# Reordering the first 13 microseconds of a fused adaLN, attention and MLP kernel, and moving TensorE's branch behind its last matmul

## Chip, cores, metric

One core of one Trainium2 chip. The metric is device microseconds of the whole launch. Engines in profile lines: PE is TensorE (PEld its weight loads), DVE is VectorE, ACT is ScalarE, POOL is GpSimd, SP is SyncE; a "q" behind the name is the engine's sequencer. Tiles in them: st, mv and rstd are row statistics, tmp and sc_bf the steps of silu, xn normalized rows, modc scale and shift, hT the transposed input of q, PT the output rows, wmw weights (in the opening those of w_mod); psQ, psS, psO and psW are TensorE's output banks. Dummies are psW<-ones, and a psO ahead of q.

## The reference, cut to what matters

```python
mod = (silu(c) @ w_mod).reshape(1, 6, 1, 512)        # c: 512 values, w_mod: 512 x 3072
sa, ca, ga, sb, cb, gb = (mod[:, i] for i in range(6))
h = layernorm(x) * (1 + ca) + sa                     # x: 2048 x 512, bf16
x = x + ga * attention(h, k_cache, v_cache, wq, wo)  # 32 heads of 128, 8 kv heads, last 512 keys
h = layernorm(x) * (1 + cb) + sb
out = x + gb * (relu(h @ w1) @ w2)                   # 512 -> 1792 -> 512
```

Before the first attention score, four things must have happened for the first 512 rows of x: the row statistics, the normalization (tiles 0 to 3, 128 rows each), the products of w_mod with silu(c), and q = h @ wq. That is the **opening**. From then on TensorE streams matmuls to the end.

## The kernel before

Each engine has its own list of operations; a helper works out the semaphore waits between them. The dummy matmuls, `warm`, only keep TensorE busy so that its clock turns up. The opening, cut:

```python
    warm(7)                                   # 7 dummies of 512 columns
    silu_exp(5)                               # TensorE transposes c; ScalarE: exp(-c) and a copy
    warm(9)
    # ... ScalarE: mean and variance of tile 3
    silu_mul()                                # GpSimd: 1 + exp(-c), its power -1, the product with c
    ln_stat(0); ln_stat(1)                    # VectorE
    rstd_add(0, 2); rstd_pow(0, 2)            # VectorE, then GpSimd: (var + eps) ** -0.5
    ln_stat(2); rstd_add(2, 3); rstd_pow(2, 4)
    ln_norm(0); ln_norm(1)                    # VectorE; tile 3 is normalized by GpSimd
    ln_tposes(0, TB[0])                       # TensorE: four 128 x 128 transposes
    for f in mod_cols_mm(0, QBK): f()         # TensorE: 32 products of one column
    ln_norm(2)
    mod_cols_evac(0, QBK)                     # VectorE: scale and shift out of PSUM
    for tl in range(1, TPB): ln_tposes(tl, TB[tl // 2])
    mod_half(0, 0, DVE); mod_half(0, 2, ACT)  # a piece of hT: transposed tiles * scale + shift
    # ... the other pieces of hT, 16 q matmuls in halves, copies to SBUF
```

Once, late in the program, every engine reads a flag (was the softmax safe without its maximum?) and branches: either the rest of its fast list, or a general kernel of thousands of instructions that lies in between in the program:

```python
            def engine(name, e):
                stream, n_ops = fast[name], cut[name]
                kb.emit(stream, e, 0, n_ops)
                e.wait_ge(sems[flag_ev[0]], flag_ev[1])
                v = e.value_load(flag[0:1, 0:1])
                with e.If(v != 128):
                    # ... the rest, then the whole general kernel
                with e.Else():
                    kb.emit(stream, e, n_ops)
```

TensorE's `cut` stood two groups before the end of the third block of the MLP, at about 510 us.

## Time and profile before

| | before |
|---|---|
| time | 560.52 us median of 3 runs (560.2 to 560.57) |
| span of the profiled run | 559.4 us (this run timed at 561.1 us) |
| TensorE busy | 98% of the span |
| first q matmul | 10.86 us |
| copy of the first q ends | 12.98 us |
| last matmul starts | 556.47 us |
| issue of the last output to its landing | 1.49 us |

The opening and the tail are read in the chain and in the timeline; in between, TensorE's stream is one block.

### The profile page before, as it was taken

The numbers are of one execution on the slowest core, as the hardware profiler recorded it, in microseconds if no ns is written. First come the engines' busy times: TensorE is split into PE (matmuls) and PEld (weight loads), VectorE is DVE, ScalarE is ACT, GpSimd is POOL, SyncE is SP. The second block draws the span as 40 slices with busy tenths as digits, with TensorE's granted clock in tenths as the row PEclk, the third lists the DMA queues.
The fourth block names the chain that finished last, engine by engine and source line by source line (L and its number), as shares of the span: only waits on it lengthen the run. The fifth ranks groups of instructions, "written<-read, shape, count | busy, mean of one in ns | idle before, by whom it ended". The sixth has DMA issues, their size and how long they took to land.

```text
span 559.4 us, 9666 instructions
## 1 busy us (share of the span) xinstructions
PE 550.5 (98%) x4060; PEld 315.8 (56%) x4134; DVE 253.8 (45%) x551; ACT 348.9 (62%) x453; POOL 54.7 (10%) x53
## 2 busy tenths in 40 slices
PE   8999999999999999999999999999999999999998
PEld 4665555555555555555555555555555654444444
DVE  4455555553546544335445443333354448321134
ACT  4986666666666666666666666666666644432500
POOL 3000022004410000033000000332000000000000
DMA  9897763513114144352352412111215110210001
GB/s 268 248 207 174 143 169 46 114 39 76 40 38 76 39 73 117 58 133 57 94 95 57 76 40 39 39 39 38 39 39 76 39 30 0 44 34 23 22 29 47
DMA packets 113309, 42.67 MB, mean 76 GB/s; under 512 B 93928, under 2 KB 112104, under 8 KB 113256
## 3 DMA queue, kind: packets, MB, share of 16 engines
q1 hardware_dynamic: 112024, 40.82, 34.3%
q10 hardware_dynamic: 1232, 1.15, 0.6%
q8 instruction: 33, 0.54, 0.4%
q14 instruction: 20, 0.16, 0.1%
HBM read 18.35 MB, written 2.10 MB: 37 GB/s over the span
## 4 chain that ended last, share of the span: by engine, by line
PE 98%; issue 1%; DMA 1%; DVE 0%; SPq 0%; DVEq 0%
PE psS L1372 28%; PE psO L1372 27%; PE psQ L1372 23%; PE psW L1372 20%; DMA c_row<-in_c_dram 1%; DVE qT L1611 0%; DVE hT L1630 0%; SPq L1303 0%; DVE PT L1723 0%; DVE PT L1725 0%; PE psS L1375 0%; PE psO L1416 0%; DVE modc L1438 0%; DVEq L123 0%
## 5 line engine op out<-in xcount | busy, mean ns | idle before, releaser
L1493 ACT ACTIVATE PT<-psS 128x1024 bf16<-128x1024 f32 x256 | 262.7, 1028 | 128.2 <-PE psS L1372 128.1
L1372 PE MATMUL psS<-qT,kT 128*128 128x512 bf16 x508 | 150.9, 379 | 0.5 <-DVE qT L1611 0.4
L1372 PEld LDWEIGHTS psO<-v,PT 128*128 128x128 bf16 x2048 | 126.6, 98 | 30.2
L1372 PE MATMUL psO<-v,PT 128*128 128x129 bf16 x2048 | 137.0, 220 | 0.0
L1372 PE MATMUL psQ<-hT,wq 128*128 128x512 bf16 (+1 forms) x510 | 130.5, 377 | 0.3 <-DVE hT L1630 0.2
L1503 DVE RECIPROCAL rinv<-psO 128x4 f32<-128x4 f32 x128 | 23.3, 182 | 227.2 <-PE psO L1372 227.2
L1372 PE MATMUL psW<-wo,oT 128*128 128x512 bf16 x454 | 118.1, 379 | 3.0
L1504 DVE TENSOR_TENSOR o<-psO,rinv 128x512 bf16<-128x512 f32 x128 | 88.5, 691 | 4.9 <-DVE rinv L1503 0.5
L1372 PEld LDWEIGHTS psQ<-hT,wq 128*128 128x128 bf16 x512 | 49.9, 98 | 60.3 <-issue 0.6
L1372 PEld LDWEIGHTS psS<-qT,kT 128*128 128x128 bf16 x512 | 49.5, 98 | 58.9 <-ACT PT L1493 0.7
L1485 ACT ACTIVATE qT<-psQ 128x512 bf16<-128x512 f32 x126 | 74.7, 593 | 0.0
L1712 ACT ACTIVATE wq<-psS 128x512 bf16<-128x512 f32 x56 | 33.4, 597 | 49.3 <-PE psS L1372 48.9
L1372 PEld LDWEIGHTS psW<-wo,oT 128*128 128x128 bf16 x512 | 45.0, 98 | 32.9 <-DVE acc L1526 1.2
L1526 DVE TENSOR_TENSOR acc<-psW,acc 128x512 f32<-128x512 f32 x48 | 33.2, 691 | 6.5 <-PE psW L1372 6.5
L1372 PE MATMUL psO<-wmw,wq 128*128 128x512 bf16 (+1 forms) x165 | 32.8, 352 | 0.3
L1529 POOL TENSOR_TENSOR acc<-acc,gaf 128x512 f32<-128x512 f32 x12 | 15.6, 1303 | 146.7 <-DVE acc L1526 139.8
L1388 POOL TENSOR_TENSOR rstd<-rstd,cst 128x4 f32<-128x4 f32 x7 | 7.2, 1025 | 216.8 <-DVE rstd L1387 216.8
L1723 DVE TENSOR_TENSOR PT<-psO,gbf 128x512 f32<-128x512 f32 (+1 forms) x12 | 7.5, 624 | 40.4 <-PE psO L1372 40.4
L1372 PE MATMUL psS<-h2T,wmw 128*128 128x512 bf16 x109 | 25.0, 379 | 0.2
L1372 PEld LDWEIGHTS psO<-wmw,wq 128*128 128x128 bf16 x168 | 15.3, 98 | 16.5
L1372 PE MATMUL psS<-hT,wmw 128*128 128x512 bf16 x110 | 24.4, 379 | 0.1
L1382 DVE BATCH_NORM_STATS2 st<-x 128x6 f32<-128x512 bf16 x31 | 21.1, 681 | 4.8 <-DMA x<-in_A_x_dram 4.8
(85 smaller groups left out, 192.6 us busy)
## 6 DMA issues: line engine op xcount, KB each, us to landing
wo<-in_A_wo_dram SPq DMA_DIRECT2D x4, 1024.0 KB, 5.9
wq<-in_A_wq_dram SPq DMA_DIRECT2D x7, 512.0 KB, 4.6
wmw<-in_B_w_dram SPq DMA_DIRECT2D x14, 256.0 KB, 3.1
wmw<-in_w_mod_dram SPq DMA_DIRECT2D x5, 512.0 KB, 4.8
oT<-o SPq DMA_TRANSPOSE x128, 2.4
out_dram<-PT SPq DMA_DIRECT2D x15, 128.0 KB, 1.7
x<-in_A_x_dram SPq DMA_DIRECT2D x3, 512.0 KB, 4.3
v<-in_A_v_cache_dram SPq DMA_DIRECT2D x8, 128.0 KB, 3.8
```

Of the source, the lines that this page charges most:

```text
L1372: kb.op(PE, lambda e: e.matmul(out_ap, lhsT, rhs, start=start, stop=stop), reads=reads, group_writes=[R_b[k] for k in bk], signal=signal)
L1382: kb.op(DVE, lambda e: e.bn_stats(st[:, t, :], x_sb[:, t, :]), reads=[R_x[t]], writes=[R_st[t]])
L1388: kb.op(POOL, lambda e: e.tensor_tensor(rstd[:, sl], rstd[:, sl], cst[:, 0:1].to_broadcast([P, hi - lo]), op=ALU.pow), reads=R_rstd[sl] + ...
L1485: kb.op(ACT, lambda e: e.activation(qT[u % NQT][:, :], bank[bk], ACTF.Copy), reads=[R_b[bk]], writes=[R_qT[u % NQT]])
L1493: kb.op(ACT, lambda e: e.activation(PT[u % NPT][:, pr * 2:pr * 2 + 2, :], s_ps[pr][:, :, :], ACTF.Exp, scale=scale), reads=[R_b[pr * 2], R ...
L1503: kb.op(DVE, lambda e: e.reciprocal(rinv[:, u, :], o_ps[:, :, P]), reads=[R_b[5], R_b[6]], writes=[R_rinv])
L1504: kb.op(DVE, lambda e: e.tensor_tensor(o_sb[u % NOS][:, :, :], o_ps[:, :, 0:P], rinv[:, u, :].unsqueeze(2).to_broadcast([P, TPB, P]), op=A ...
L1526: kb.op(DVE, lambda e: e.tensor_tensor(acc[:, tl, :], bank[WBK], acc[:, tl, :], op=ALU.add), reads=[R_b[WBK], R_acc[tl]], writes=[R_acc[tl]])
L1529: kb.op(eng, lambda e: e.tensor_tensor(acc[:, tl, :], acc[:, tl, :], gaf[:, :], op=ALU.mult), reads=[R_acc[tl], R_ga], writes=[R_acc[tl]])
L1712: kb.op(ACT, lambda e: e.activation(h1T[b % 2][:, fc, :], bank[bk], ACTF.Relu), reads=[R_b[bk]], writes=[R_h1[b % 2][fc]], pre=all_events( ...
L1723: kb.op(DVE, lambda e: e.tensor_tensor(yt[i][:, c0:c1], bank[bk][:, c0:c1], gbf[:, c0:c1], op=ALU.mult), reads=[R_b[bk], R_gb], writes=[R_ ...
```

## The change

Its intent: get silu off GpSimd so that the powers for rstd start sooner, spread the normalizations over three engines, let the products go first, shape the dummies so that they do not hold back real work, and take TensorE's branch out of its busy time. It also moves other transfers: the first two heads' wq goes in two pieces on the SP queue instead of one on ACT's, and the first keys are issued ahead of the next two heads' wq. The memset of `ones` goes from GpSimd to VectorE. The core of the diff:

```diff
     def silu_mul():
-        # three operations on POOL, the second a power
+        # the same on DVE, the second a reciprocal
     def load_wm01(i, eng=None):
-        # two halves of w_mod's first 1024 columns, 512 KB each
+        # four quarters, alternating between the ACT and SP queues
-    warm(7)
+    warm(8)
     silu_exp(5)
-    warm(9)
...
-    silu_mul()
     ln_stat(0)
+    warm(3, [R_mv[0]])          # waits for the statistics of tile 0
     ln_stat(1)
+    warm(2, [R_mv[1]])          # and of tile 1
     rstd_add(0, 2)
     rstd_pow(0, 2)
+    # POOL: -mean * rstd of tile 1;  ACT: normalization of tile 1
+    silu_mul()
     ln_stat(2)
     rstd_add(2, 3)
     rstd_pow(2, 4)
     ln_norm(0)
-    ln_norm(1)
...
-    ln_tposes(0, TB[0])
     fs = mod_cols_mm(0, QBK)
     for f in fs:
         f()
-    ln_norm(2)
+    ln_tposes(0, TB[0])
     mod_cols_evac(0, QBK)
-    for tl in range(1, TPB):
-        ln_tposes(tl, TB[tl // 2])
+    ln_tposes(1, TB[0])
+    warm(2, bk=6)
     mod_half(0, 0, DVE)
     mod_half(0, 2, ACT)
+    ln_norm(2)
+    ln_tposes(2, TB[1])
+    ln_tposes(3, TB[1])
+    warm(1, bk=6)
...
-                mlp.insert(len(mlp) - 2, lambda: cut_here("pe"))
...
     assert not tasks and not bgq and not wo_ready
+    cut_here("pe")
```

More of the change, by code (lines that the diff above doesn't have):

```diff
@@ L1319, in build_fast @@
     R_q1 = RL("q1_", 2)
+    R_wmc = RL("wmc", DC)
+    R_wqa = RL("wqa", 2)
+    R_nmr = Res("nmr")
     R_cf, R_m01 = Res("cf"), Res("m01")
@@ L1350, in load_wm01 @@
     def load_wm01(i, eng=None):
-        c0, c1 = i * DC // 2, (i + 1) * DC // 2
-        dma(wm01[:, c0:c1, :], wm01v[:, c0:c1, :], f"wm{i}", writes=[R_wm[i]], eng=eng)
+        dma(wm01[:, i, :], wm01v[:, i, :], f"wmc{i}", writes=[R_wmc[i]], eng=eng)
     def wm_res(sl, cc):
-        return R_wm[cc // (DC // 2)] if sl < 2 else R_wm[sl]
+        return R_wmc[cc] if sl < 2 else R_wm[sl]
     def load_wo(j):
@@ L1363, in load_mlp @@
         if not wm_done:
-            wm_done.extend(all_events(R_wm))
+            wm_done.extend(all_events(R_wm + R_wmc))
         f0 = i % (FC // 2) * 2
@@ L1375, in tpose, with warm @@
         kb.op(PE, lambda e: e.transpose(out_ap, in_ap, ident[:, :]), reads=list(reads) + [R_ident], group_writes=[R_b[k] for k in bk], signal=signal)
-    def warm(n):
+    def warm(n, gate=(), bk=7):
         for i in range(n):
-            mm(bank[WBK], ones[:, :], ones[:, 0:1].to_broadcast([P, QB]), True, True, [R_ones], [WBK], i == n - 1)
+            mm(bank[bk], ones[:, :], ones[:, 0:1].to_broadcast([P, QB]), True, True, [R_ones] + list(gate), [bk], i == n - 1)
     def ln_stat(t):
@@ L1420, in silu_mul @@
     def silu_mul():
-        kb.op(POOL, lambda e: e.tensor_scalar(tmp[:, :], tmp[:, :], 1e38, 1.0, op0=ALU.min, op1=ALU.add), reads=[R_tmp], writes=[R_tmp])
-        kb.op(POOL, lambda e: e.tensor_tensor(tmp[:, :], tmp[:, :], cst[:, 3:4].to_broadcast([P, DC]), op=ALU.pow), reads=[R_tmp, R_eps], writes=[R_tmp])
-        kb.op(POOL, lambda e: e.tensor_tensor(sc_bf[:, :], c_f[:, :], tmp[:, :], op=ALU.mult), reads=[R_tmp, R_cf], writes=[R_sc])
+        kb.op(DVE, lambda e: e.tensor_scalar(tmp[:, :], tmp[:, :], 1e38, 1.0, op0=ALU.min, op1=ALU.add), reads=[R_tmp], writes=[R_tmp])
+        kb.op(DVE, lambda e: e.reciprocal(tmp[:, :], tmp[:, :]), reads=[R_tmp], writes=[R_tmp])
+        kb.op(DVE, lambda e: e.tensor_tensor(sc_bf[:, :], c_f[:, :], tmp[:, :], op=ALU.mult), reads=[R_tmp, R_cf], writes=[R_sc])
     def mod_cols_mm(which, bk):
@@ L1480, in q_mms @@
             mm(bank[bk], wq_sb[:, cc, h * Dh:(h + 1) * Dh], hT[b % 2][:, cc, :], i == 0, i == DC - 1,
-               [R_wq[h], R_hT[b % 2][cc]] + ([R_h0[cc]] if b == 0 else []), [bk], i == DC - 1)
+               (R_wqa if h < QA else [R_wq[h]]) + [R_hT[b % 2][cc]] + ([R_h0[cc]] if b == 0 else []), [bk], i == DC - 1)
         q_evac(u, bk)
@@ L1561, in build_fast @@
     dma(c_row[:, :], c[0].rearrange("(c p) -> c p", p=P), "c", writes=[R_c])
-    load_wm01(0)
-    load_wm01(1, ACT)
-    load_wq(0, 2, ACT)
+    for i in range(DC):
+        load_wm01(i, (ACT, SP)[i % 2])
+    for i, eng in enumerate((SP, SP)):
+        dma(wq_sb[:, 2 * i:2 * i + 2, 0:QA * Dh], wqv[:, 2 * i:2 * i + 2, 0:QA * Dh], f"wqa{i}", writes=[R_wqa[i]], eng=eng)
+    load_k(0)
     load_wq(2, 2)
-    load_k(0)
     load_v(0)
-    kb.op(POOL, lambda e: e.memset(ones[:, :], 1.0), writes=[R_ones])
+    kb.op(DVE, lambda e: e.memset(ones[:, :], 1.0), writes=[R_ones])
     kb.op(POOL, lambda e: e.memset(cst[:, 0:1], -0.5), writes=[R_cst])
@@ L1592, in rstd_pow @@
               reads=R_rstd[lo:hi] + [R_cst], writes=R_rstd[lo:hi])
-    silu_mul()
     ln_stat(0)
+    warm(3, [R_mv[0]])
     ln_stat(1)
+    warm(2, [R_mv[1]])
     rstd_add(0, 2)
     rstd_pow(0, 2)
+    kb.op(POOL, lambda e: e.tensor_scalar(s3[:, 3:4], mv[:, 1, 0:1], rstd[:, 1:2], -1.0, op0=ALU.mult, op1=ALU.mult), reads=[R_mv[1], R_rstd[1]], writes=[R_nmr])
+    kb.op(ACT, lambda e: e.activation(xn[:, 1, :], x_sb[:, 1, :], ACTF.Identity, bias=s3[:, 3:4], scale=rstd[:, 1:2]),
+          reads=[R_x[1], R_nmr, R_rstd[1]], writes=[R_xn[1]])
+    silu_mul()
     ln_stat(2)
@@ L1636, in q_half @@
             mm(bank[bk][:, hf * HB:(hf + 1) * HB], wq_sb[:, cc, u * Dh:(u + 1) * Dh], hT[0][:, cc, hf * HB:(hf + 1) * HB], cc == CC_ORDER[0], cc == CC_ORDER[-1],
-               [R_wq[u], R_half[hf][cc]], [bk], cc == CC_ORDER[-1])
-    for tl in range(1, TPB):
-        ln_tposes(tl, TB[tl // 2])
+               [R_wqa[cc // 2], R_half[hf][cc]], [bk], cc == CC_ORDER[-1])
+    ln_tposes(1, TB[0])
+    warm(2, bk=6)
     mod_half(0, 0, DVE)
     mod_half(0, 2, ACT)
+    ln_norm(2)
+    ln_tposes(2, TB[1])
+    ln_tposes(3, TB[1])
+    warm(1, bk=6)
     mod_half(0, 1, DVE)
@@ L1712, in h1_group @@
         kb.op(ACT, lambda e: e.activation(h1T[b % 2][:, fc, :], bank[bk], ACTF.Relu), reads=[R_b[bk]], writes=[R_h1[b % 2][fc]],
-              pre=all_events(R_wq) if b < 2 else ())
+              pre=all_events(R_wq + R_wqa) if b < 2 else ())
     def y_group(b, tl, c0=0, c1=D, deng=None):
```

## The prediction

> **What bounds the kernel now.** I read the page first. Its busy shares and its chain of work that ended last say the same thing:
>
> ```profile
> PE 550.5 (98%) x4060; PEld 315.8 (56%) x4134; DVE 253.8 (45%) x551; ACT 348.9 (62%) x453; POOL 54.7 (10%) x53
> ...
> PE 98%; issue 1%; DMA 1%; DVE 0%; SPq 0%; DVEq 0%
> ```
>
> TensorE is the path for 98% of the span. A busy TensorE need not be at its peak, so I took the starts of successive matmuls from the timeline. From 13.3 us on, full-width ones (512 columns) start 0.216 us apart and 128-column ones 0.056 us apart, almost without exception. Nearly every longer step is one whole extra 0.216 us, at regular intervals: a missing record, not a stall. So from 13.3 us to the last matmul near 556.5 us TensorE streams without a break, and the change does not touch that work. What can move is **when the stream starts, at what clock, one hiccup inside it, and the tail**.
>
> The second view was the chain of waits over the first 14 us:
>
> ```profile
> 1.24 3.66 DMA c_row<-in_c_dram
> 4.90 0.05 issue
> 4.95 0.18 PE psO L1416
> 5.13 3.86 PE psW L1372 x9
> 8.98 0.22 PE psS L1375 x4
> 9.21 0.79 PE psQ L1372 x32
> 10.00 0.02 issue
> 10.02 0.18 DVE modc L1438
> ...
> 10.30 0.42 DVE hT L1630
> ...
> 12.55 0.44 DVE qT L1611
> 12.99 0.35 issue
> ```
>
> Columns are start, length, what. The nine psW matmuls are dummies that only keep TensorE busy. They end at 8.98 us and hold back the transposes and the 32 products, although the inputs of both were there earlier: the VectorE row of the timeline has the first normalized tile at 8.23 us, and the second half of the modulation weights landed at 7.91 us. Only then follow modulation (10.2 us), the halves of hT, the first q, its copy (to 12.98 us), and the stream.
>
> Third, the timeline of the engines that feed this (GpSimd above, VectorE below; start, length, engine, line, operation):
>
> ```profile
> 5.80 1.04 POOL L1422 TENSOR_TENSOR tmp<-tmp,cst 128x4 f32<-128x4 f32 x1
> 6.92 0.20 POOL L1423 TENSOR_TENSOR sc_bf<-c_f,tmp 128x4 bf16<-128x4 f32 x1
> 7.08 1.51 POOL L1591 TENSOR_TENSOR rstd<-rstd,cst 128x2 f32<-128x2 f32 x2
> 8.70 0.90 POOL L1604 TENSOR_SCALAR xn<-x,s,rstd 128x512 bf16<-128x512 bf16 x1
> ...
> 6.53 0.17 DVE L1588 TENSOR_SCALAR rstd<-mv 128x2 f32<-128x2 f32 x1
> 6.60 0.69 DVE L1382 BATCH_NORM_STATS2 st<-x 128x6 f32<-128x512 bf16 x1
> ...
> 7.82 1.22 DVE L1393 TENSOR_SCALAR xn<-x,mv,rstd 128x512 bf16<-128x512 bf16 x3
> ```
>
> GpSimd finishes silu at 7.12 us, so the first power for rstd, whose input was ready at 6.69 us, starts at 7.08.
>
> **What the Trainium skill says.** "TensorE: Matmul & The Clock Gate", Part 1, says that TensorE runs at half clock until about 3.4 us of sustained activity inside a free-running window. The trace agrees: dummies start 0.427 us apart from 1.04 us on, still at 8.02 us, then the step shrinks (0.374 us) and everything after 8.8 us runs at 0.216 us per 512 columns. Part 4 there says that transposes do not count as activity for this; no row here shows it. "Runtime: NRT & Kernel Launch", Instruction fetch mechanics, says a taken branch breaks the sequential prefetch of instructions. The trace shows TensorE's branch at 510.6 us, but with a queue full of matmuls: the cost I find is the single step from 513.74 to 514.15 us. "DMA: Bandwidth & Descriptors", Issuing engines are not separate DMA queues, says DMAs of several issuers share 16 engines, so splitting the same megabyte of w_mod into quarters should not land its last byte sooner; here the two halves landed at 6.16 and 7.91 us.
>
> **Part by part.**
> 1. *Silu to VectorE.* It removes 0.28 + 1.04 + 0.20 us from GpSimd and adds three small VectorE operations (0.17 to 0.18 us each by the rows of that size, about 0.5 us in sequence) between the variance of tiles 0 and 1 (ends 6.69) and the statistics of tile 2. The first power then runs 6.73 to 7.43 instead of ending at 7.78. But VectorE is pushed back: statistics of tile 2 at 7.1 instead of 6.6, its variance at 8.2 instead of 7.7, so the second power starts at 8.22 instead of 7.77, and GpSimd's own tile (0.90 us) ends near 10.0 instead of 9.6. This part costs 0.4 us on the last tile.
> 2. *Tile 1 on ScalarE.* A small GpSimd product (0.28) after the power, then one activation (0.65 to 0.72 by the rows of 512 columns): 7.76 to 8.45. It lies beside the rest. It takes one of three normalizations (about 0.33 us apart) from VectorE. Tile 0 ends near 8.5 rather than 8.23, because VectorE reaches it later.
> 3. *Products first.* Dummies now come as 8, then 3 behind the statistics of tile 0 (5.70) and 2 behind those of tile 1. At half clock the five take 5 x 0.427 from 5.80 to 7.93. The 32 products start then, with the last weights just in, and at full clock take 0.79, to 8.7; modulation is ready near 9.1, where it was 10.2. That removes 1.1 us from the old chain.
> 4. *What takes its place.* Behind modulation stand now the transposes of tiles 0 and 1 (2 x 0.22, to 9.1), the first pieces of hT on VectorE and ScalarE (from 9.35), and only after the first VectorE piece the normalization of tile 2 (9.67 to 10.08). TensorE then does two dummies, the transposes of tiles 2 and 3 (the latter waiting until about 10.1 for GpSimd's tile), one dummy, and q from about 10.86, the very time at which it starts now. Its first four matmuls no longer wait for ScalarE in between (11.36 now), so they end some 0.25 us sooner. The second half of hT waits for the transposes of tile 3 (10.82): five VectorE pieces at 0.32 us pitch become three, ending at 11.9 instead of 11.99. The 12 remaining q matmuls at 0.109 follow, and the copy ends near 12.8 instead of 12.98. **Gain 0.2 us**, not 1.1: tiles 2 and 3 have become the wait.
> 5. *The branch behind the last matmul.* The step 513.74 to 514.15 is 0.41 where 0.216 is normal: **gain 0.19 us**. At the end TensorE's load and branch (about 0.5 us of load, then a wait for the drain) follow the last matmul at 556.7. The last output lands at 558.87, so some 2 us of slack hides them.
> 6. *DMA order.* The w_mod quarters keep their volume; keys and value rows keep theirs. The first keys landed at 9.78 and are needed at 13, so a microsecond of delay there is free.
>
> Sum: 560.52 - 0.2 - 0.19 = **about 560.1 us**.
>
> **Rivals.**
> *The clock stays low.* Now nine dummies run without a break from 5.06 to 8.98, and the clock rises at about 8.77. The new opening has eight (3.4 us, ending about 4.3) and then a burst of only 2.1 us before products that are mostly weight loads, and transposes. If the flip slips by one window of 3.4 us, to about 12.2, the products take perhaps 1.6 instead of 0.8, each set of transposes doubles, and 16 q matmuls cost 0.213 instead of 0.109: 1.5 to 2 us, so about 562; two windows would add another 1 to 2. For it: the first seven dummies, followed by a pause, did not raise the clock in this trace. Against it: the eighth dummy, the products and the extra dummies may fill a window, and the count looks tuned. I give it one in four.
> *The full microsecond comes through.* If the second half hides in VectorE's and ScalarE's pace and GpSimd's tile comes early, the stream starts 1 us sooner: 559.3. Against it: the normalization of tile 2 is placed behind the first piece of hT. One in eight.
> *The tail grows.* A jump over the unused general kernel right at the end could miss its instructions, with no queue of matmuls to hide it. Against it are those 2 us of slack; if the fetch exceeds them, +0.5 us or so, 560.6. One in ten.
>
> **Range and chances.** The likely case is 559.8 to 560.4. The good rival sets the lower end, 559.2, the clock the upper, 562.0. The span of the prize is at most 13 us of opening, of which 2% would be 11 us: neither direction can reach it, short of a wrong transfer order that stalls the stream. So faster 0.005, same 0.985, slower 0.01.
>
> **What would show it right or wrong.** The timeline should show the first power at 6.7, products at 7.9 in steps of 0.025 us, modulation near 9.1, the first q at about 10.9 and the first score matmul about 12.9. The single long step at 514 should be gone, and the branch should end before the last output has landed. If dummies or q matmuls at 9 us or later step by 0.427 (or 0.213 for 256 columns), the clock rival holds. If the first score matmul comes at 12 us, I overrated the wait for tiles 2 and 3; if the products wait for w_mod, the order of transfers decides.

## The result, and the profile after

The changed kernel took **562.23 us median of 5 runs (561.22 to 563.53)** against 560.20 us for the kernel before in the same rounds (559.97 to 560.57): ratio 1.0037, 95% interval 1.0016 to 1.0058. A ratio is the mean time of one kernel's fast runs over that of the other's of the same rounds, so it is not quite the ratio of the medians. Within 2% it is "the same", but it is slower, and outside my range.

The five runs are 561.22, 561.24, 562.23, 563.32 and 563.53. Those of the kernel before keep within 0.6 us here (within 0.9 to 1.7 us in the sets of the experiments below, which have 9 to 11 runs of it). The profile after is that of the 561.24 run, one of the two quick ones. The page's busy shares and chain by engine:

```profile
PE 549.1 (98%) x4060; PEld 315.5 (56%) x4134; DVE 254.1 (45%) x554; ACT 349.9 (63%) x454; POOL 53.3 (10%) x50
...
PE 97%; DVE 1%; issue 1%; DMA 1%
```

Nothing of the bulk has moved. The chain over the opening of the changed kernel (start, length, what):

```profile
4.60 0.71 DVE st L1384
...
6.82 0.16 DVE sc_bf L1425
...
8.00 0.34 DVE xn L1395
8.33 0.04 issue
8.38 0.64 PE psS L1377 x8
...
9.04 0.41 DVE hT L1635
9.45 0.48 DVE xn L1395
9.92 0.05 issue
9.97 0.34 PE psS L1377 x3
...
10.59 0.22 PE psO L1374
10.80 0.44 PE psQ L1374 x4
11.24 0.89 PE psO L1374 x8
12.13 0.02 issue
12.15 0.44 DVE qT L1617
```

The chain no longer passes through the first dummies and the products. It is VectorE's: statistics, silu, statistics of tile 2, tile 0 (8.00), transposes, a piece of hT, and only then tile 2 (9.45), the transposes of tiles 2 and 3, a dummy (psO, 10.59) and q. The copy of the first q ends at 12.58 instead of 12.98 us. The dummies and the products in TensorE's timeline:

```profile
5.57 1.40 PE L1374 MATMUL psW<-ones 128*128 128x512 bf16 x5 [0.62 <-DVE mv L1385]
7.04 1.17 PE L1374 MATMUL psQ<-sc_bf,wmw 128*128 128x1 bf16 x32
```

Five dummies in 1.40 us are full-clock dummies: in this run the clock had turned up at 3.94 us, and the products start at 7.04 us.

At the other end, TensorE's branch. In the view by source line, of the kernel before and then of the changed one (count, shortest/median/longest in ns, start):

```profile
L1830 PEldq COMPARE_BRANCH  x1: 3440/3440/3440, 510.6 to 510.6; - x1
```

```profile
L1839 PEldq COMPARE_BRANCH  x1: 3394/3394/3394, 555.7 to 555.7; - x1
```

It takes 3.4 us in both places. And the outputs issued while it runs, in the list of DMA issues over the last microseconds of the changed kernel (size, time from issue to landing):

```profile
q8 instruction: 1, 0.02, 1.3%
issues: line engine op xcount, KB each, median us to landing
out_dram<-PT ACTq DMA_DIRECT2D x1, 64.0 KB, 1.6
out_dram<-PT SPq DMA_DIRECT2D x1, 32.0 KB, 2.8
out_dram<-PT ACTq DMA_DIRECT2D x1, 32.0 KB, 2.2
```

The two last outputs took 2.8 and 2.2 us to land; before, the same two took 1.45 and 1.49. In the same stretch stands one transfer on the instruction queue, 16 KB. The kernel before has none there; its own stands beside its branch, at 511.63 us. The other four engines' records of the same branch, in the same view, are 0.05 to 0.07 us long; why TensorE's alone is long no run here shows.

So the span can be cut into four terms, each read from the trace: when the first statistics start (x has landed), from there to the end of the copy of the first q, from there to the start of the last matmul, and from there to the end.

| us | x landed | opening | stream | tail | span |
|---|---|---|---|---|---|
| before (561.1 us run) | 4.79 | 8.19 | 543.49 | 2.89 | 559.36 |
| after (561.24 us run) | 4.60 | 7.98 | 543.29 | 3.61 | 559.48 |

Opening and stream have each gained 0.2 us, as predicted. The tail has lost 0.72. That accounts for these two runs. It does not account for runs of 562 to 563.5 (the 563.32 us run even lists a clock of 1.0, and its cause was never seen), nor for the kernel before being usually quicker than its own profiled run.

### The profile page after: what moved, and what is told of

The parts are those of the page before. It is cut to its first block, busy times and chain, and to the rows that moved or that the text cites. A ratio compares the mean times of both kernels' runs of the same rounds, so it can differ in the third digit from the quotient of the medians.

```text
span 559.5 us, 9671 instructions
## 1 busy us (share of the span) xinstructions
PE 549.1 (98%) x4060; PEld 315.5 (56%) x4134; DVE 254.1 (45%) x554; ACT 349.9 (63%) x454; POOL 53.3 (10%) x50
## 4 chain that ended last, share of the span: by engine, by line
PE 97%; DVE 1%; issue 1%; DMA 1%
PE psS L1374 28%; PE psO L1374 27%; PE psQ L1374 22%; PE psW L1374 19%; DMA x<-in_A_x_dram 1%; DVE st L1384 0%; PE psS L1377 0%; DVE xn L1395 0%; DVE mv L1385 0%; DVE qT L1617 0%; DVE hT L1635 0%; DVE rstd L1590 0%; DVE PT L1732 0%; DVE PT L1734 0%; DVE tmp L1424 0%
```

## The experiments

Two theories. **Tail**: the branch at the end costs more than it saved, because it must fetch instructions. **Clock**: the new dummies leave it to chance whether TensorE runs at full clock in the opening. A third question came up on the way: is the new order any better once the clock is steady? Every kernel gave correct results.

### again: the changed kernel once more

> The changed kernel once more, unaltered, to see its runs spread and with luck a trace of a slow one. Clock theory (the pauses between the dummies leave it to the phase of the clock's window whether TensorE runs at full clock during the opening): times again in groups from about 561.2 to 563.5 us, and the longer a run, the later the last dummy or q matmul that steps at half clock (0.427 us per 512 columns, 0.213 per 256); in a run above 562 the first score matmul starts later than 14 us, against 12.72 us in the first trace. Rival, that the loss sits in the tail: the first score matmul stays near 12.7 us in every trace and slow runs are slow after the last matmul.

Measured: 562.33 us median (561.69 to 564.21, 6 runs), ratio 1.0035 (1.0021 to 1.0048). Over both sets, 9 of 11 runs are above 561.3. This trace is of a 562.21 us run. TensorE's timeline:

```profile
5.61 2.31 PE L1374 MATMUL psW<-ones 128*128 128x512 bf16 x5 [0.74 <-DVE mv L1385]
7.72 1.04 PE L1374 MATMUL psQ<-sc_bf,wmw 128*128 128x1 bf16 x32
8.62 1.01 PE L1377 MATMUL psS<-ident,xn 128*128 128x128 bf16 x8
```

The same five dummies take 2.31 us and the eight transposes 1.01 instead of 0.62: half clock. The clock record has the turn at 9.56 us. The opening took 8.43 us against 7.98. My "later than 14 us" for the first score matmul was wrong (13.22): a late turn alone costs only some 0.45 us, by these two traces. The tail was 3.98.

### e1_branch_back

```diff
+                mlp.insert(len(mlp) - 2, lambda: cut_here("pe"))
-    cut_here("pe")
```

> The changed kernel with TensorE's branch back at its old place inside the MLP, nothing else. Tail theory (the branch at the end fetches a 16 KB page of instructions that the last two output transfers wait behind, 0.7 us, and costs more than the 0.19 us step at 514 us that it saved): a fast run loses 0.7 and pays 0.2 again, so its best runs come to about 0.5 us under the best of the changed kernel, 560.7 or a little less, and the step of 0.41 us at about 513 is back. Clock theory: the spread stays, slowest minus fastest run still 1.5 us or more. If the tail were the whole loss, all runs would lie within 0.5 us of each other and below 560.

Measured: 561.18 us median (560.73 to 563.09), ratio 1.0007 (0.9994 to 1.0020). The best run is 0.49 us under the best of the changed kernel's first set, as expected, and 0.96 under the best of `again` (the runs drew different clocks); the spread is 2.4 us. Its trace is of the slowest run, 563.09 us, and shows the clock theory's stronger form. The windows view, cut at the turns in the clock record (3.82, 10.65, 14.06) and halfway between the first two (columns: stretch, length, busy time and count by engine, clock, DMA):

```profile
3.82:7.24 3.42, 2.09 (x9) 0.42 (x6) 2.27 (x9) 2.16 (x8) 0.44 (x1) 1.00 1.02 364
7.24:10.65 3.41, 2.65 (x51) 1.98 (x52) 2.50 (x8) 1.83 (x3) 2.10 (x4) 1.00 1.30 195
10.65:14.06 3.41, 3.41 (x19) 2.28 (x17) 1.29 (x4) 1.33 (x3) 0.00 (x0) 0.50 1.15 308
```

The clock was up at 3.82 us and was **turned down again** for 3.41 us from 10.65, under the very q matmuls that it had been warmed for. In the stretch before, TensorE counts as busy 2.65 of 3.41 us, but with 32 one-column products, the first transposes and two dummies. The stretch ahead of it has less busy time (2.09), made mostly of dummies, and the clock stayed up. The opening took 9.44 us, 1.46 more than in the first trace after.

### e2_branch_only

The kernel before with only the two lines of the branch moved.

> The kernel before with only TensorE's branch moved behind its last matmul. Tail theory: the 0.41 us step disappears (minus 0.2), the branch takes about 3.4 us from its compare at about 556 us, and the last output lands some 0.7 us later after its issue than the 1.49 us of before: about 0.5 to 0.8 us slower than before, with no more spread than before has (0.6 us). My prediction's step 5 said 0.19 us faster. Clock theory alone: no change of more than 0.2 us.

Measured: 560.85 us median (560.72 to 562.30), ratio 1.0010 (0.9997 to 1.0023): 0.18 us over before, where I had expected 0.5 to 0.8. That is inside the noise of the clock, so the time decides nothing. The trace shows more: the stream is 543.29 us, the tail 3.56 (2.89 before), the last output takes 2.10 us to land. It shows something else: the **old** opening, untouched, took 7.59 us here, with the clock turned up at 6.94. The 8.19 us of the trace from which I predicted was not typical.

### e3_dummies

On top of e1_branch_back:

```diff
-    warm(8)
+    warm(9)
     silu_exp(5)
+    warm(3)
     ln_stat(0)
-    warm(3, [R_mv[0]])
     ln_stat(1)
-    warm(2, [R_mv[1]])
+    warm(3, [R_mv[1]])
...
-    warm(2, bk=6)
+    warm(4, bk=6)
```

> The kernel of e1_branch_back with the dummies made continuous: 9 instead of 8 at the start, 3 right behind the transpose of c without a wait, 3 behind the statistics of tile 1, and 4 instead of 2 between the transposes of tiles 1 and 2. Clock theory: TensorE has no pause over 0.1 us before about 7 us as long as it is at half clock, so any window phase turns the clock up by about 7.4 us; the runs stop spreading (within 0.6 us) and their median falls under that of e1_branch_back by about 1 us or more, to 559.5 to 559.9, faster than the kernel before. If the spread has another cause than the clock, it stays.

Measured: 560.74 us median (560.54 to 561.04), ratio 0.9999 (0.9986 to 1.0012). The spread fell from 2.4 to 0.5 us (0.36 in e9, the same kernel once more), and all ten runs list clock 1.0. The listed clock leaves out the time before the first turn (`again`'s traced run lists 0.999 with its turn at 9.56 us), so it says only that no run was seen turned down later. So the dummies made most of e1's spread; that they did it by way of the clock rests on the traces (e1's was turned down, e3's was not). But the median came no lower than that of the kernel before, where I had expected 559.5 to 559.9: with branch and clock both mended, the new order gains nothing. Its opening took 8.09 us, with the clock up at 4.04. The head of its chain is not VectorE's any more:

```profile
1.72 6.36 DMA wmw<-in_w_mod_dram
8.07 0.05 issue
8.12 0.56 PE psQ L1374 x16
```

The products stood still for 0.76 us until a quarter of w_mod had landed at 8.07 us. The chains of e1 and e9 begin in the same way (8.40 and 8.18).

### e4_before_dummies and e5_before_dummies_end

e4 is the kernel before with

```diff
-    warm(7)
+    warm(9)
     silu_exp(5)
-    warm(9)
+    warm(6)
...
     for tl in range(1, TPB):
+        if tl == TPB - 1:
+            warm(2, bk=6)
         ln_tposes(tl, TB[tl // 2])
```

and e5 is e4 with the branch at the end.

> The kernel before with other dummies only: 9 instead of 7 before the transpose of c, 6 instead of 9 behind it, and 2 new ones between the transposes of tiles 2 and 3. Clock theory: TensorE is busy without a pause from 1.0 to about 7.6 us while at half clock, so the clock is up by about 7.4 us at the latest, and the queue of dummies no longer reaches past the first normalized tile (8.2 us); the first score matmul comes at 12.1 to 12.5 us in each run, as in the trace of e2_branch_only with its early turn (12.29), against 13.1 in the trace of before. Median 0.3 to 0.7 us under before, spread within 0.6 us. That would mean that the old order of work opens faster than the new one (12.72 at its best). Rival (the new parts do gain, and the 12.29 was luck with the input transfer): no faster than e3_dummies was against its before.

> e4_before_dummies with TensorE's branch behind the last matmul as well, so that the tail is weighed without the spread of the clock. Tail theory: last output lands 2.1 to 2.5 us after its issue against 1.5 in e4, the middle step of 0.41 us is gone: 0.3 to 0.6 us slower than e4. Step 5 of my prediction: 0.19 us faster.

Measured: e4 560.95 us (560.78 to 560.99), ratio 1.0004; e5 561.56 us (561.43 to 563.10), ratio 1.0021 (1.0008 to 1.0035). e4 missed: I had expected 0.3 to 0.7 us under before, and it was not faster. In its trace the branch took 3.80 us in the middle and the stream 543.85, 0.29 to 0.36 more than in the two traces of before (more on that below). Its opening, 7.64 us, is near the 7.59 of e2; that is the old order's usual opening, as before_again shows below, so there was little to gain. The first score matmul came at 12.62, just outside my 12.1 to 12.5. The pair is the cleanest weighing of the tail, on one chip and with a nearly steady clock: **+0.61 us** (0.3 to 0.6 expected). Their traces agree: stream -0.56, tail +1.14. The list of DMA issues at the end, e4 and then e5:

```profile
out_dram<-PT SPq DMA_DIRECT2D x1, 32.0 KB, 1.4
out_dram<-PT ACTq DMA_DIRECT2D x1, 32.0 KB, 1.5
```

```profile
q8 instruction: 1, 0.02, 1.9%
issues: line engine op xcount, KB each, median us to landing
out_dram<-PT ACTq DMA_DIRECT2D x1, 64.0 KB, 1.6
out_dram<-PT SPq DMA_DIRECT2D x1, 32.0 KB, 3.2
out_dram<-PT ACTq DMA_DIRECT2D x1, 32.0 KB, 2.6
```

### e6_norm2_first and e7_products_first

e6 is e3 with `ln_norm(2)` moved right behind `ln_norm(0)` and 2 dummies for 4; e7 is e4 with the products ahead of `ln_tposes(0, ...)`.

> e3_dummies with the normalization of tile 2 moved on VectorE from behind the first piece of hT to right behind that of tile 0 (where the old order has it), and 2 instead of 4 dummies in the wait that this shortens. If the late tile 2 is what holds the new opening at 12.72 us (10.65 for the first q), the first q comes at 10.2 to 10.5 us and the first score matmul at about 12.4; median about 0.3 us under that of e3_dummies relative to before. If modulation or ScalarE holds it, nothing changes.

> e4_before_dummies with the 32 products ahead of the transposes of tile 0, the one reordering of the change that takes work off the old chain, with the rest of the old opening left as it was. Expected: modulation 0.1 to 0.2 us earlier than in e4, first score matmul 12.0 to 12.3 us, median 0 to 0.2 us under e4; within noise if VectorE's normalization of tile 2 (to 9.0 us) stands in front of the evacuation of the products anyway.

Measured: e6 560.61 us (560.58 to 560.65), ratio 0.9999; e7 560.72 us (560.26 to 560.82), ratio 0.9998. Neither differs from before in time (e6 was to come 0.3 us under e3 in relation to before, and both have 0.9999), but the openings do: e6 7.74 us against 8.09 in e3, e7 7.46 against 7.64 in e4. Not all of e6's 0.35 need be tile 2's: w_mod held the products until 8.12 us in e3 and until 7.90 in e6. In e7 the chain begins with w_mod's second half, landed at 8.04, and the first score matmul came at 12.50, not at 12.0 to 12.3. In e6 the first q comes at 10.43 us and the first score matmul at 12.52, 0.1 us later than I had hoped. Its chain says why:

```profile
8.12 0.81 POOL rstd L1594
8.93 0.10 issue
9.03 0.91 POOL xn L1611
9.94 0.05 issue
9.98 0.34 PE psS L1377 x3
```

With tile 2 out of the way, GpSimd's tile 3 is the wait. It is late because its power waits for VectorE's variance, which silu has pushed back.

### e8_mixed, e9_new_again, e10_old_again

e8 keeps of the change what I took to have helped, and the rest as before; against the changed kernel:

```diff
     # silu_mul on POOL and ahead of ln_stat(0), ones on POOL, ln_norm(1) on DVE, cut_here("pe") in the middle: as before
-    warm(8)
+    warm(9)
     silu_exp(5)
-    # warm(3, [R_mv[0]]), warm(2, [R_mv[1]])
+    warm(6)
...
     mod_cols_evac(0, QBK)
+    ln_norm(2)
     ln_tposes(1, TB[0])
-    warm(2, bk=6)
     mod_half(0, 0, DVE)
     mod_half(0, 2, ACT)
-    ln_norm(2)
+    warm(2, bk=6)
     ln_tposes(2, TB[1])
     ln_tposes(3, TB[1])
-    warm(1, bk=6)
```

e9 is e3 and e10 is e4, unaltered, on e8's chip.

> Meant to beat both: silu on GpSimd, tile 1 on VectorE and the branch in the middle as in the kernel before; from the change the w_mod quarters and the products ahead of the transposes, the evacuation of the products now ahead of the normalization of tile 2; dummies 9, 6 and 2 as in e4. Products can start at about 7.2 us and modulation is ready near 8.8. From the landing of x to the copy of the first q I expect 7.2 to 7.5 us (7.46 in e7_products_first, 7.98 in the changed kernel, 8.19 in the kernel before): 0.2 us under e10_old_again and 0.4 to 0.6 under e9_new_again, and 0 to 0.5 us under the kernel before.

> e3_dummies unaltered, on the same chip as e10_old_again, to set the new opening against the old one with the clock steady in both and the branch at the old place in both. If the new order is itself no faster at full clock (8.09 us from x to the copy of the first q in e3 against 7.64 in e4), it is 0.2 to 0.5 us slower than e10_old_again here; if the parts of the change gain once the clock is steady, as step 4 of my prediction had it (0.2 us), it is faster.

> e4_before_dummies unaltered, as the partner of e9_new_again. Its times should lie within 0.3 us of each other; TensorE's branch takes 3.4 to 3.8 us from its compare, of which what exceeds 3.24 us shows as the long step in the middle, so up to 0.4 us of difference between these two can come from there and is to be taken off by the traces.

Measured, with 560.66 us for the kernel before (560.43 to 561.28): e8 **560.22** (560.11 to 560.82), ratio 0.9993 (0.9979 to 1.0006); e9 561.11 (561.01 to 561.37), 1.0005; e10 560.92 (560.79 to 562.41), 1.0002. So e9 is 0.19 us slower than e10 in the medians, which the branch in the middle can make up by itself (3.84 us in e9's trace, 3.62 in e10's, a difference of 0.22), and e8 0.44 us faster than before, with an interval that still holds 1. e8's opening took 7.08 us, the shortest of all and under the 7.2 to 7.5 that I expected; its chain:

```profile
2.05 5.89 DMA wmw<-in_w_mod_dram
7.94 0.05 issue
7.99 0.35 PE psQ L1374 x8
8.34 0.51 PE psS L1377 x8
...
9.89 0.44 PE psQ L1374 x4
```

The last quarter of w_mod is what this opening waits for. No run tries the w_mod quarters or the new order of transfers by themselves, so what they are worth stays open. e10's slow run, which is its trace, corrects a belief of mine: the clock was up at 6.24 and down again from 9.65 to 13.06, so e4's dummies are not proof against every phase.

### before_again

> The kernel before, unaltered, for a second trace. Its trace on which I predicted took 8.19 us from the landing of x to the copy of the first q, with the clock turned up only at about 8.8 us, and ran at 561.1 us, above the 559.97 to 560.57 of the timed runs. If that was an unlucky phase of the clock, this trace, if it comes from a run near 560.5, takes about 7.6 us, as in e2_branch_only, whose opening is the same, with modulation ready at about 9.3 to 9.4 instead of 10.19. If the phase makes no such difference to the old opening, it takes 8.2 us again.

Measured: 561.04 us median (560.64 to 561.72), 1.0004 against itself, so some 0.05% is noise here. The trace, of a 560.70 us run, has an opening of 7.63 us. TensorE's timeline in it:

```profile
5.13 2.13 PE L1372 MATMUL psW<-ones 128*128 128x512 bf16 x9
8.35 0.40 PE L1375 MATMUL psS<-ident,xn 128*128 128x128 bf16 x4 [1.10 <-DVE xn L1393]
```

The nine dummies that took 3.86 us in the prediction's chain take 2.13 here, and TensorE then waits 1.10 us for tile 0. The dummies hold nothing back when the clock turns up early.

### All traces side by side

| us | opening | branch | stream | tail |
|---|---|---|---|---|
| before / before_again | 8.19 / 7.63 | 3.44 / 3.50 | 543.49 / 543.56 | 2.89 / 2.89 |
| after / again | 7.98 / 8.43 | 3.39 / 3.77 at the end | 543.29 / 543.29 | 3.61 / 3.98 |
| e1_branch_back | 9.44 | 3.96 | 544.16 | 2.88 |
| e2_branch_only | 7.59 | 3.33 at the end | 543.29 | 3.56 |
| e3_dummies / e9 | 8.09 / 7.97 | 3.66 / 3.84 | 543.71 / 543.90 | 2.87 / 2.87 |
| e4_before_dummies / e10 | 7.64 / 9.02 | 3.80 / 3.62 | 543.85 / 543.67 | 2.89 / 2.89 |
| e5_before_dummies_end | 7.73 | 3.81 at the end | 543.29 | 4.03 |
| e6_norm2_first | 7.74 | 3.44 | 543.49 | 2.87 |
| e7_products_first | 7.46 | 3.74 | 543.80 | 2.89 |
| e8_mixed | 7.08 | 3.62 | 543.67 | 2.88 |

Read the stream column against the branch column. With the branch at the end the stream is 543.29 us in each of four traces. With the branch in the middle it is longer by the branch's time minus 3.24 us, to 0.01 us in nine traces of ten (e4: 0.56 and 3.80 - 3.24; e6: 0.20 and 3.44 - 3.24). In e1, where the clock was down until shortly before the stream, it is 0.15 more. So some 3.24 us of queued matmuls, 15 of 0.216 us, hide the branch, and only the rest shows.

The branch's own time follows its fetch. In each of the fourteen traces one 16 KB packet on the instruction queue starts 0.98 to 1.14 us after the branch, and takes from 0.96 us (e2, branch 3.33) over 1.27 (again, 3.77) to 1.56 (e1, 3.96). What is left of the branch is 2.38 to 2.53 us in all fourteen. That this packet is the code which the branch jumps to is inferred from that. And where the branch stands at the end, the tail is its time plus 0.21 to 0.23 us. So the move to the end costs about 0.57 us however long the branch takes (an estimate from these sums: 0.22 + 3.24 - 2.89), close to the 0.61 measured.

## Why the prediction was wrong

**Step 5 failed, in its second half.** "At the end TensorE's load and branch (about 0.5 us of load, then a wait for the drain) follow the last matmul at 556.7 ... some 2 us of slack hides them." The first half held: the middle step vanished and gave 0.20 us. But the branch is no wait for the drain. It takes 3.3 to 4.0 us wherever it stands, and its time follows that of one 16 KB transfer on the instruction queue. I had cited the page "Runtime: NRT & Kernel Launch" on taken branches and had then explained the cost away with the queue of matmuls, although the 3.44 us record lay in the trace: I took its end, just behind the last queued matmul, for its cause. The 2 us of slack did not cover it: at the end the branch starts 0.14 us before the last matmul does, and TensorE is done only at 559.13 us in the first trace after. The program ends 0.36 us behind that, in each of the four traces with the branch at the end. Beside it the outputs are late too: the last one lands 0.6 to 1.1 us longer after its issue than in before, the one ahead of it 1.3 to 1.7. The two delays do not add up; the outputs alone, which elsewhere land 0.49 us before the end, would have put it only 0.04 to 0.05 us sooner (an estimate). "DMA: Bandwidth & Descriptors", Queues, rings and completion order, says that each DMA engine drains a whole packet of one queue before it turns to the next; the traces agree as far as they go: the 16 KB packet takes 0.96 us (e5: 1.43) on one engine, and the last few output packets come out after it has ended. That their wait is for that one engine is argued, not tried. The net cost is shown: +0.61 us (e5 against e4) where I had -0.19. My rival "the tail grows" had the mechanism; I gave it one in ten and +0.5 us on the sum, and the tail grew by 0.72.

**The rival "the clock stays low" was, by the times, the usual case (9 of 11 runs above 561.3), not one in four.** Its mechanism holds (again: turn at 9.56 us, dummies at 0.427 us). Its size and a part of its form do not. The late turn cost 0.45 us of opening, not 1.5 to 2: it came at 9.56 us and not at 12.2, ahead of q, and the products hardly feel the half clock (32 take 0.87 us from first to last start in `again`, 0.78 at full clock in before). What costs 1.4 to 1.5 us is a form I had not thought of: a clock that is up and is **turned down again** for 3.41 us, under the first q (e1, e10). That the waits between products, transposes and first q held too few full-width matmuls fits both traces, and e3's added dummies, but is not shown apart. The chance of it was underrated because I counted dummies before the products and none of the pauses after them.

**Steps 1 to 4 had the right mechanisms, measured from a wrong base.** Step 1 said that silu on VectorE would cost the last tile 0.4 us: tile 3 ended 4.81 us behind x in before (9.60 - 4.79) and 5.17 behind it after (9.77 - 4.60), 0.36 later. Step 2's activation took 0.81 us instead of at most 0.72. In step 3 the products came at 7.04 in the early-clock run and at 7.72 in the late-clock one, not at 7.93. Step 4 named tiles 2 and 3 as the new wait, and e6 showed it (8.09 to 7.74 with tile 2 moved, w_mod's part in this set aside). The sum of these, an opening 0.2 us shorter than in the trace of before, was met, 0.21, by luck: the trace of before had its clock late, the trace after had it early. Late against late the new opening is 0.24 us longer (again, 8.43 against 8.19), and against the usual 7.6 us (before_again, e2) the new opening, 8.0 us with the clock up, is 0.35 to 0.4 us **longer**, by single traces. The warning was in the numbers that I had: a profiled run of 561.1 us beside timed runs of 560.2 to 560.57.

**What adds up.** On one chip: 562.33 (again), 561.18 with the branch back (e1), 560.74 with dummies that keep the clock up (e3), 560.67 for before. Of the first step, 1.15 us, some 0.6 is the tail by e5 against e4; the remainder I put down to the clock (all six runs of `again` list 0.992 to 0.999, e1's two 0.997 and three 1.0), which is argued. How the chances of the clock's phases share the rest between e1 and e3 can't be fixed with so few runs, and stays open. The kernel before is not free of it: three of its runs in the later sets, 561.84 to 562.00 us, list 0.997. Why the same 16 KB take 0.96 us in one run and 1.56 in another is open too.

**Step 6 held for the keys, not for w_mod.** The first keys landed at 9.28 us, needed at 12.7. The last quarter of w_mod landed at 7.81 us in the trace after (7.91 before) and held nothing up there; but with the products first it became the head of the chain in e1, e3, e7, e8 and e9, where it or the part that was missing landed at 7.94 to 8.40. My own sign, "if the products wait for w_mod, the order of transfers decides", had come up, and I did not follow it with a run.

## What to carry to other kernels

When one engine is busy 98% of the time, take the trace apart into arrival, opening, stream and tail, and check first that the profiled run is a usual one: a trace of an unlucky run makes a wrong base for a right sum. A taken branch over a large block of instructions took 3.3 to 4 us on TensorE here, whatever stood around it; put it where queued matmuls cover it and where no output is in flight, which is the middle of a stream, not its end. In this opening dummy matmuls had to cover the pauses between real work, not only the time before it, and even e4's did not in every run (e10); a spread of runs is as much a result as their median.

## What the Trainium skill lacked or had wrong

- "TensorE: Matmul & The Clock Gate", in its table "Why this matters for your kernels", warns only of idle gaps over about 3 us (its "A second HAM failure mode" tells of short pauses in another kernel, without their share of the time). Here the clock was turned down after a stretch in which no pause exceeded 0.5 us and the profile counted TensorE busy for 2.65 of 3.41 us (e1, 7.24 to 10.65). One-column products and transposes seem to count for little; the page says so of transposes only.
- The same page gives no rate for one-column products at half clock: 32 with their weight loads took 0.87 us from first to last start in `again`, 0.78 at full clock in before.
- "Runtime: NRT & Kernel Launch", Instruction fetch mechanics, calls the stall of a taken branch expensive and gives no number. On TensorE it was 3.33 to 3.96 us over fourteen traces, the time of one 16 KB instruction packet (0.96 to 1.56 us) plus 2.38 to 2.53 us; a queue of 512-column matmuls hid 3.24 us of it.
- No page says whether such a fetch can hold up a kernel's own transfers: two 32 KB outputs landed 2.1 to 3.2 us after their issue with a 16 KB instruction transfer beside them, 1.45 to 1.49 us without (that it is the cause is argued).
